# Linear attention and MoE on one core: w_in laid out by tiles, v loaded without its zero rows, and one folded step in another order of products

## The chip, the core and the metric

The kernel runs on one core of one Trainium2 chip. The metric is device time in microseconds: the median of 3 runs, 1050.9 us before the change (1047.07 to 1051.64).

## What is computed

```python
def phi(x):
    proj = np.einsum('bhsd,df->bhsf', x, w_phi)
    proj = proj - np.max(np.abs(proj), axis=-1, keepdims=True)
    return np.concatenate([np.exp(proj), np.exp(-proj)], axis=-1)
q_p, k_p = phi(q), phi(k)                       # q, k, v: 8 x 8 x 576 x 64
kv  = np.einsum('bhsf,bhsd->bhfd', k_p, v)
z   = np.sum(k_p, axis=2)
num = np.einsum('bhsf,bhfd->bhsd', q_p, kv)
den = np.einsum('bhsf,bhf->bhs', q_p, z)[..., None] + 1e-06
x   = (num / den).transpose(0, 2, 1, 3).reshape(4608, 512)
h   = x @ w_in                                  # 512 x 2048, float64
out = (h - np.tanh(h)) @ w_out                  # 2048 x 512, float64
```

## The kernel before

The program has two stages, both in an order written out by hand; the scheduler keeps it.

**Attention** (the first 290 us). Two heads of one batch form a unit, 32 units in all. `period(i)` works on unit i and finishes steps of units i-1 to i-4: projections of q and k (line 246), less their maximum (`t`, lines 257 and 260), exponentials, `kv` products (line 305), numerator and denominator (361, 376), transposes (270), and on the way the decoding of one weight tile from its 8-byte floats (`dec_0` to `dec_3`). SP issues nearly all loads and stores, in the order of the program: in a period the load of q and k (`qk`, line 229), in some periods the store of a split w_out tile (`wod`, 108) and of a decoded w_in tile (`wdi`, 520), then the reciprocal of the denominator (`rr`, 404), the load of v (233), a raw weight tile (`raw`, 175 or 180), the finished x (`xs`, 419) and the spread of the reciprocal over partitions (two `rb`, 411). One DMA of the period is issued by ACT: `den_recip_load`, `dn<-dd` (395), which stands behind the copy `kv` (342) and one exponential (283), and ahead of the next period's `t` (260).

Every DMA has one of eight completion counters, DMAHW0 to DMAHW7. They are taken in turn in the order of the program, by SP's and ACT's DMAs alike, and a DMA is issued only when the last one on its counter has landed (the wait is left out where an earlier wait of the same engine implies it). A period has eight DMAs, nine with a `wdi` store, ten with a `wod` store as well.

In the v load the array `v5` has 5 blocks of 128 rows; the first 64 rows of block 0 are zeros, and each load brings all 128 x 640 values into a buffer from a pool of two. A w_in load brings a tile of 512 x 128 values, in 512 pieces of 1,024 bytes; a w_out load brings 128 rows of 4,096 bytes.

**MoE** (from 290 us on). 9 groups of 512 tokens, 8 steps each, so steps 0 to 71. Steps 0 to 15 (`plain`) multiply directly. From step 16 on the step is folded: seven smaller products (`product`, line 791) into the PSUM banks W, V, Y and X are combined by additions on DVE. `q(old)` and `q(one)` are the output products (lines 713 and 719) of sets finished before: `high` uses `gh`, `low` uses `gl`, which POOL makes. The flag `joined` puts the products 3 and 2 (into Y) ahead of `q(old)` and product 4 (into X) behind `q(one)`; without it they stand between the two:

```python
joined = s > NP * FOLD and s != NS - 1
if joined:
    for n in (3, 2):
        product(r[n], g, j, n)
```

NP * FOLD is 16, so step 16 is not joined, and steps 17 to 70 are.

Of the kernel before, what the change touches and what calls it, by code (L numbers as in the profile page):

```python
# [8 lines left out]
F32 = mybir.dt.float32  # L9
# [10 lines left out]
P = 128  # L20
# [12 lines left out]
def tile_linear_attention_moe(  # L33
# [10 lines left out]
    nc = tc.nc  # L44
    B, H, S, D = dims
    F = w_phi.shape[1]
    DM, DFF = w_in.shape
    NHP = H // 2
    NJ = S // P
    SM = NJ * P  # L50
    SR = S - SM
# [3 lines left out]
    TPP = 2 * S // P  # L55
    PC = 2 * S
    NCT = DM // P
    NF = DFF // P
    CH = S // 2
    NP = NF // 2  # L60
    GT = 4
# [16 lines left out]
    xs = [dram.tile([NHP, P, S], F32, name=f"xs{b}") for b in range(B)]  # L78
    wod = [dram.tile([P, 2, DM], F32, name=f"wod{f}") for f in range(NF)]

# [5 lines left out]
    EARLY = [t for k in range(NO) for t in (("i", 2 * k), ("o", k), ("i", 2 * k + 1))]  # L86
    LATE = [("i", f) for f in range(NI, NF)] + [("o", f) for f in range(NO, NF)]
    NE = len(EARLY)
    SEQ = [t for e, l in zip(EARLY, LATE) for t in (e, l)] + LATE[NE:]
    wd = {f: dram.tile([P, DM], F32, name=f"wdi{f}") for f in range(NI)}  # L90
    HOME = {("i", f): f for f in range(NI, NF)} | {("o", f): f - NI for f in range(NI, NF)}

# [51 lines left out]
    with ExitStack() as c1:  # L144
        raw = c1.enter_context(tc.tile_pool(name="raw", bufs=2))
        p1 = c1.enter_context(tc.tile_pool(name="p1", bufs=1))
        p2 = c1.enter_context(tc.tile_pool(name="p2", bufs=2))
# [21 lines left out]
        def dec_load(n):  # L169
            u = Dec()  # L170
            u.side, u.f = SEQ[n]
            u.nm = f"{u.side}{u.f}"
            u.r = raw.tile([P, DM], U64, tag="raw", name=f"raw{u.nm}")
            if u.side == "i":
                nc.sync.dma_start(
                    u.r.rearrange("p (c f) -> p c f", f=P),
                    w_in[:, u.f * P : (u.f + 1) * P].rearrange("(c p) f -> p c f", p=P),
                )
            else:
                nc.sync.dma_start(u.r, w_out[u.f * P : (u.f + 1) * P, :])  # L180
            return u
# [39 lines left out]
        def load(u):  # L221
            u.qk = p2.tile([P, PC], F32, tag="qk", name=f"qk{u.i}")
            cuts = [(0, PC)]
            if u.i < 2:
                cuts = [(4 * P, PC), (0, 4 * P)]
            if u.i == 0:
                cuts = [(4 * P, 5 * P), (5 * P, PC), (0, 4 * P)]
            for o, w in cuts:
                nc.sync.dma_start(u.qk[:, o:w], qkT[u.i][:, o:w])

        def load_v(u):
            u.v = p2.tile([P, 5, 2, D], F32, tag="v", name=f"v{u.i}")
            nc.sync.dma_start(u.v.rearrange("p j e d -> p (j e d)"), v5[u.i])

        ROUNDS = ((4,), (5, 6, 7, 8), (0, 1, 2, 3))

# [185 lines left out]
        for i in range(B * NHP):  # L422
            u = Unit()
# [3 lines left out]
        NU = len(units)  # L427
        assert NU == 2 * NF
        load(units[0])
        wph = p1.tile([P, F], F32, name="wph")  # L430
        nc.scalar.dma_start(wph[0:D, :], w_phi)
        nc.scalar.dma_start(wph[D:P, :], w_phi)
        load(units[1])
        load_v(units[0])
        dec = [dec_load(0), dec_load(1)]
        def unit(i):
            return units[i] if 0 <= i < NU else None
# [169 lines left out]
    with ExitStack() as c2, tc.manual_schedule():  # L607
# [6 lines left out]

        for f in range(NF):
            if f not in hl:
# [10 lines left out]
        FOLD = 2  # L627
        steps = [(g, j) for g in range(NG) for j in range(NP)]
        NS = len(steps)
# [119 lines left out]
        def wo_fetch(g, j):  # L749
            for f in (2 * j, 2 * j + 1):  # L750
                wo[g, f] = wo_load(f)
# [31 lines left out]
        def product(o, g, j, n):  # L783
            h, l = weights(j, n)
            x = xc[g][n]
            i = 0
            for c in range(2):
                k = slice(c * P, (c + 1) * P)
                m = slice(c * HN, (c + 1) * HN)
                for w, a in ((h, 0), (h, 1), (l, 0)):  # L790
                    nc.tensor.matmul(o, w[:, k], x[:, a, m], start=(i == 0), stop=(i == 5))  # L791
                    i += 1
# [91 lines left out]
        def do(s, where):  # L884
            for fn, args in jobs.pop((s, where), ()):
                fn(*args)
# [3 lines left out]
        for k, ts in enumerate(LOWS):  # L890
            for t in ts.split():
                t = t[0], int(t[1:])
                job(k, "a1", split_hi, *t)
                job(k + 1, "v0", split_lo, *t)
        for j in range(NP):
            s = NP + j
# [45 lines left out]
        for s in range(NS + 3):  # L942
            one, two, old = sets.get((s - 1, 0)), sets.get((s - 1, 1)), sets.get((s - 2, 1))
            g, j = steps[s] if s < NS else (None, None)
            fold = g is not None and g >= FOLD
            if s >= NS:
                two = None
            begun = two is not None and steps[s - 1][0] < FOLD
            do(s, "d")
            if g is not None:  # L950
                Y, X = (ps_x.tile([P, GN], F32, tag=t, name=f"y{s}" if a == 0 else f"x{s}") for a, t in enumerate("yx" if fold or s % 2 else "wv"))
                if g:
                    wo_fetch(g, j)
                new, nxt = (Set(s, a, h, (2 * j, 2 * j + 1) if fold else (2 * j + a,), (2 * a, 2 * a + 1) if fold else (0, 1, 2, 3)) for a, h in enumerate((Y, X)))
                sets[s, 0], sets[s, 1] = new, nxt
            if fold:
                W, V = (ps_x.tile([P, GN], F32, tag=t, name=f"{t}{s}") for t in "wv")
                r = {1: W[:, lo_], 6: W[:, hi_], 2: Y[:, lo_], 3: Y[:, hi_], 4: X[:, lo_], 5: V[:, lo_], 7: V[:, hi_]}
                K = gp.tile([P, 3, HN], F32, tag="k", name=f"k{s}")
                u3 = K[:, 2, :]  # L960
                for n in (1, 6, 5, 7):
                    product(r[n], g, j, n)
                nc.scalar.copy(K[:, 0, :], r[1])
                joined = s > NP * FOLD and s != NS - 1
                if joined:
                    for n in (3, 2):
                        product(r[n], g, j, n)
            elif g is not None:
                plain(Y, g, 2 * j)
            if s != NS - 1:  # L970
                q(old)
            finish(2)
            do(s, "a")
            if not begun:
                run(two, "mk_")
            finish(4)
            run(two, "d3", "d4")
            if not fold:
                run(two, "d5")
            do(s, "v0")  # L980
            do(s, "d1")
            do(s, "p0")
            if fold:
                tt(u3, r[6], K[:, 0, :], ALU.add)
                tt(K[:, 1:3, :], V.rearrange("p (a n) -> p a n", a=2), u3.unsqueeze(1).broadcast_to([P, 2, HN]), ALU.add)
                if not joined:
                    for n in (3, 2):
                        product(r[n], g, j, n)
                    if s == NS - 1:
                        q(old, (0,))  # L990
                    product(r[4], g, j, 4)
                    if s == NS - 1:
                        q(old, (1,))
            elif g is not None:
                plain(X, g, 2 * j + 1)
            q(one)
            if fold:
                tt(Y, Y, K[:, 0:2, :].rearrange("p a n -> p (a n)"), ALU.add)  # L998
                tt(X[:, hi_], r[5], u3, ALU.add)
                if joined:  # L1000
                    product(r[4], g, j, 4)
                else:
                    tt(r[4], r[4], u3, ALU.add)
                run(two, "d5")
            if g is not None:
                run(new, "y_", "s1_", "s2_")
            run(two, "gh_", "gl_")
            if g is not None:
                run(new, "th_", "mk_", "d1", "d2")
                if fold and joined:  # L1010
                    tt(r[4], r[4], u3, ALU.add)
                if (s, "p1") in jobs:
                    nc.gpsimd.tensor_copy(mark, new.s1[:, 0:1])
                    do(s, "p1")
                run(new, "d3", "d4", "d5")
                do(s, "v1")
                if s == NS - 1:
                    nxt, end = (Set(s, f"1{k}", X[:, cols], (2 * j + k,), (2, 3), k == 1) for k, cols in enumerate((lo_, hi_)))
                    sets[s, 1], sets[s + 1, 1] = nxt, end
                run(nxt, "y_", "s1_", "s2_")  # L1020
                run(new, "gh_", "gl_")
                run(nxt, "th_", "d1", "d2")
                if not fold or s == NS - 1:
                    run(nxt, "mk_")
                if s == NS - 1:
                    run(nxt, "d3", "d4", "d5")
                    run(end, "y_", "s1_", "s2_")
                    run(nxt, "gh_", "gl_")
                    run(end, "th_", "mk_", "d1", "d2", "d3", "d4", "d5", "gh_", "gl_")
            do(s, "v")  # L1030
            do(s, "a1")
# [56 lines left out]
```

## Time and profile before

| | us |
|---|---|
| median of 3 runs | 1050.9 |
| the profiled execution | 1050.99 |
| its span, first to last instruction | 1049.2 |
| PE busy | 1030.6 (98%) |
| DVE, ACT, POOL busy | 935.3, 860.8, 486.7 |

The span is what the profile's rows divide; the execution's own time is 1.8 us longer. TensorE's granted clock is 0.999 of full speed over the span. Times in rows count from the span's start. PE is the matmul row of TensorE, PEld its weight loads; SPq and ACTq are the queues' own instructions, such as DMA issues.

### The profile page before, as it was taken

What the parts mean: (1) busy time and instruction counts of PE and PEld (TensorE: products, weight loads), DVE (VectorE), ACT (ScalarE), POOL (GpSimd) and SP (SyncE); (2) the same over time, 40 slices, a digit from 0 to 9 for tenths busy, and PEclk for the clock granted to TensorE, in tenths of its full rate; (3) what the DMA queues carried; (4) which work ended last, traced back from release to release, by engine and by line L of the source; (5) the groups of instructions that cost most, each with busy time, mean ns of one, the idle gap of its engine ahead of it and who ended that gap; (6) DMA issues with size and microseconds to landing.
All of it is one profiled execution on the core that took longest, in us unless ns stands there. A gap on an engine that the chain in (4) does not pass through costs nothing.

```text
span 1049.2 us, 24806 instructions
## 1 busy us (share of the span) xinstructions
PE 1030.6 (98%) x9476; PEld 855.8 (82%) x9476; DVE 935.3 (89%) x1457; ACT 860.8 (82%) x1580; POOL 486.7 (46%) x347
## 2 busy tenths in 40 slices
PE   8999999999999999999999999999999999999997
PEld 5666666666678888888989898999989898999986
DVE  7999999998989989998888888888888888888886
ACT  6999999998988877778878778777878777877766
POOL 4555555555324434434443553553463553553232
PEclk9999999999999999999999999999999999999999
DMA  6788888888633363343325325234325324332423
GB/s 206 205 269 245 259 248 266 248 258 249 190 117 124 116 222 125 101 138 105 119 97 185 109 93 201 82 121 162 120 93 188 109 94 154 129 121 81 161 89 112
DMA packets 76214, 165.55 MB, mean 158 GB/s; under 512 B 16704, under 2 KB 31296, under 8 KB 76096
## 3 DMA queue, kind: packets, MB, share of 16 engines
q1 hardware_dynamic: 71896, 163.63, 48.5%
q8 instruction: 75, 1.23, 0.5%
q10 hardware_dynamic: 4200, 0.34, 0.3%
q14 instruction: 43, 0.35, 0.1%
HBM read 134.28 MB, written 29.51 MB: 156 GB/s over the span
## 4 chain that ended last, share of the span: by engine, by line
PE 79%; DVE 9%; ACT 6%; DMA 4%; issue 1%; ACTq 0%; SPq 0%; DVEq 0%; POOL 0%; POOLq 0%
PE po L713 22%; PE po L719 11%; PE y L791 7%; PE w L791 7%; PE v L791 7%; PE pp L305 5%; PE po L361 4%; PE x L791 4%; PE y L800 3%; PE x L800 3%; PE pp L376 2%; ACT qe L283 1%; DMA rb<-rr 1%; DVE m L251 1%; ACT t L260 1%
## 5 line engine op out<-in xcount | busy, mean ns | idle before, releaser
L686 POOL TENSOR_TENSOR gl<-s,gh 128x512 fp32r<-128x512 f32 x144 | 223.6, 1553 | 417.7 <-ACT gh L682 297.5
L713 PE MATMUL po<-wo,gh 128*128 128x512 f32 x1152 | 302.5, 391 | 1.0 <-ACT gh L682 1.0
L713 PEld LDWEIGHTS po<-wo,gh 128*128 128x128 f32 x1152 | 211.8, 188 | 44.0 <-ACT gh L682 2.3
L719 PE MATMUL po<-wo,gl 128*128 128x512 f32 x576 | 169.9, 389 | 0.0
L647 ACT ACTIVATE y<-y 128x512 f32<-128x512 f32 x72 | 43.2, 600 | 114.5 <-DVE y L998 108.8
L315 POOL TENSOR_TENSOR ss<-kp 128x1024 f32<-128x1024 f32 (+1 forms) x32 | 73.6, 2299 | 118.3 <-DVE rb L416 89.9
L678 DVE COPY_PREDICATED s<-mk,th 128x512 f32<-128x512 uint32 x144 | 118.6, 823 | 9.5 <-ACT s L651 0.5
L719 PEld LDWEIGHTS po<-wo,gl 128*128 128x128 f32 x576 | 108.0, 188 | 22.6 <-DVE gl L686 0.2
L666 DVE SCALAR_TENSOR_TENSOR s<-s,y 128x512 f32<-128x512 f32 x144 | 99.5, 691 | 29.3 <-ACT s L651 29.2
L669 DVE SCALAR_TENSOR_TENSOR s<-s,s 128x512 f32<-128x512 f32 x144 | 104.1, 723 | 15.3 <-ACT gh L682 0.5
L651 ACT ACTIVATE s<-y,bias_t 128x512 f32<-128x512 f32 x144 | 104.2, 723 | 14.3 <-DVE s L672 9.3
L663 ACT ACTIVATE mk<-y,bias_t 128x512 f32<-128x512 f32 x144 | 103.7, 720 | 0.0
L655 ACT ACTIVATE s<-y,bias_t 128x512 f32<-128x512 f32 x144 | 101.9, 708 | 0.0
L251 DVE TENSOR_REDUCE m<-pp 128x8 f32<-128x1024 f32 (+1 forms) x96 | 90.8, 952 | 11.2 <-PE pp L246 9.9
L295 ACT ACTIVATE kp<-t 128x1024 f32<-128x1024 f32 (+1 forms) x128 | 87.6, 733 | 8.7 <-DVE t L257 7.9
L682 ACT CAST gh<-s 128x512 fp32r<-128x512 f32 (+1 forms) x145 | 88.4, 610 | 7.3 <-DVE s L678 4.6
L791 PE MATMUL y<-xc,hl 128*128 128x256 f32 x672 | 85.4, 275 | 1.1 <-DVE th L675 1.1
L791 PEld LDWEIGHTS y<-xc,hl 128*128 128x128 f32 x672 | 80.5, 188 | 1.3 <-issue 1.2
L305 PE MATMUL pp<-kp,v 128*32 128x256 f32 x1240 | 73.3, 381 | 7.7 <-ACT t L260 5.9
L257 DVE TENSOR_TENSOR t<-pp,m 128x1024 f32<-128x1024 f32 x64 | 78.4, 1225 | 2.3
L791 PE MATMUL w<-xc,hl 128*128 128x256 f32 x560 | 79.9, 277 | 0.0
L246 PE MATMUL pp<-wph,qk 64*128 64x128 f32 x1152 | 74.4, 277 | 1.6 <-issue 1.2
(142 smaller groups left out, 2187.5 us busy)
## 6 DMA issues: line engine op xcount, KB each, us to landing
wo<-wod SPq DMA_DIRECT2D x128, 512.0 KB
qk<-in_qkT SPq DMA_DIRECT2D x30, 576.0 KB
v<-in_v SPq DMA_DIRECT2D x32, 320.0 KB
rb<-rr SPq DMA_DIRECT2D x64, 144.0 KB
xs<-rb SPq DMA_DIRECT2D x32, 288.0 KB
out<-xco SPq DMA_DIRECT2D x35, 256.0 KB
rawi<-in_moe_w_in SPq DMA_DIRECT2D x16, 512.0 KB
rawo<-in_moe_w_out SPq DMA_DIRECT2D x16, 512.0 KB
```

The lines of the kernel that those rows point to most:

```text
L251: nc.vector.tensor_reduce(u.m, u.x, AX.X, ALU.max, apply_absolute_value=True, negate=True)
L305: nc.tensor.matmul(u.pc[o : o + HD, 0 : 2 * F], u.v[:, j, e, h * HD : (h + 1) * HD], u.kp[:, e, j, :, :], start=(a == 0), stop=(a == 4))
L651: nc.scalar.activation(self.s1, self.y, AF.Square, bias=bias_t[:, 0:1])
L655: nc.scalar.activation(self.gs, self.y, AF.Square, bias=bias_t[:, 1:2])
L663: nc.scalar.activation(self.mk, self.y, AF.Relu, bias=bias_t[:, 2:3])
L666: stt(self.s1, self.s1, PC1, self.y, ALU.add, ALU.mult)
L669: stt(self.s1, self.gs, PC2, self.s1, ALU.add, ALU.mult)
L678: nc.vector.copy_predicated(self.gs, self.mk.bitcast(U32), self.th)
L686: (nc.vector if self.spare else nc.gpsimd).tensor_tensor(self.gl, self.gs, f32(self.gh), ALU.subtract)
L713: nc.tensor.matmul(po[g, t], v.gh[:, cut], wo[g, f][:, k, :], start=not begun, stop=False)
L719: nc.tensor.matmul(po[g, t], v.gl[:, cut], wo[g, f][:, 0, :], start=False, stop=last and f == v.fs[-1])
L791: nc.tensor.matmul(o, w[:, k], x[:, a, m], start=(i == 0), stop=(i == 5))
```

## The change

w_in is laid out on the host as 16 tiles of 128 x 512 values, so that a tile is one block of 128 rows of 4,096 bytes, in the order that the load wanted in SBUF before. v is loaded in two DMAs that leave out the 64 zero rows of block 0: rows 64 to 127 whole (64 x 640 values), rows 0 to 63 without block 0 (64 x 512). The buffers are two fixed tiles whose zero part POOL writes once, at the start. Step 17 is no longer joined.

```diff
-    DM, DFF = w_in.shape
+    NF, DM = w_in.shape[0], w_out.shape[1]
...
-                nc.sync.dma_start(
-                    u.r.rearrange("p (c f) -> p c f", f=P),
-                    w_in[:, u.f * P : (u.f + 1) * P].rearrange("(c p) f -> p c f", p=P),
-                )
+                nc.sync.dma_start(u.r, w_in[u.f])
...
         def load_v(u):
-            u.v = p2.tile([P, 5, 2, D], F32, tag="v", name=f"v{u.i}")
-            nc.sync.dma_start(u.v.rearrange("p j e d -> p (j e d)"), v5[u.i])
+            u.v = vb[u.i % 2]
+            t = u.v.rearrange("p j e d -> p (j e d)")
+            nc.sync.dma_start(t[SR:P, :], v5[u.i, SR:P, :])
+            nc.sync.dma_start(t[0:SR, 2 * D :], v5[u.i, 0:SR, 2 * D :])
...
+        vb = [p1.tile([P, 5, 2, D], F32, name=f"v{b}") for b in range(2)]
+        for t in vb:
+            nc.gpsimd.memset(t[0:SR, 0], 0.0)
...
-                joined = s > NP * FOLD and s != NS - 1
+                joined = s > NP * FOLD + 1 and s != NS - 1
...
-        "moe_w_in": inputs["moe_w_in"],
+        "moe_w_in": _np.asarray(inputs["moe_w_in"]).reshape(H * D // W, W, -1, W).transpose(2, 1, 0, 3).reshape(-1, W, H * D),
```

SP's DMAs of period 13 and the head of period 14, before, with the counters that each waits for:

```order
L229 DMA qk15_2118<-in_qkT 128x1152 [waits DMAHW5_49,PE_49]
L108 DMA wod1_81<-wo1_1800 128x1024
L520 DMA wdi3_105<-dwi3_2037 128x512 [waits DMAHW7_49]
L404 DMA rr10_2190<-rn10_2191 128x9 [waits DMAHW0_49,DVE_49]
L233 DMA v14_2195<-in_v5 128x640 [waits DMAHW1_49,PE_49]
L175 DMA rawi14_2202<-in_moe_w_in 128x4x128 [waits DMAHW2_49,DVE_49,Activation_49]
L419 DMA xs2_74<-rb9_2078 128x576 [waits DMAHW4_49,DMAHW3_49,DVE_49]
L411 DMA rb10_2241<-rr10_2190 64x576 [waits DMAHW0_49]
```

The same place with the change:

```order
L225 DMA qk15_2122<-in_qkT 128x1152 [waits PE_49]
L107 DMA wod1_81<-wo1_1804 128x1024 [waits DMAHW4_49]
L521 DMA wdi3_105<-dwi3_2041 128x512 [waits DMAHW5_49]
L402 DMA rr10_2194<-rn10_2195 128x9 [waits DMAHW6_49,DVE_49]
L230 DMA v0_146<-in_v5 64x640 [waits DMAHW7_49,PE_49]
L231 DMA v0_146<-in_v5 64x512 [waits DMAHW0_49]
L174 DMA rawi14_2206<-in_moe_w_in 128x512 [waits DMAHW1_49,DVE_49,Activation_49]
L417 DMA xs2_74<-rb9_2082 128x576 [waits DMAHW2_49,DVE_49]
L409 DMA rb10_2245<-rr10_2194 64x576 [waits DMAHW6_49,DMAHW3_49]
```

The DMA of `qk15` was on counter 5 and is now on 3; `wod1` was on 6 and is now on 4, and one more DMA stands between it and `xs2`.

ACT at the end of the same period, before (`dn11` is the DMA that ACT issues, `t14` the next unit's first instruction):

```order
L287 ACTIVATE qe12_2207<-ptr12_2208 128x2x64
L342 COPY kv12_2206<-ptk12_2210 128x384 [waits PE_49]
L283 ACTIVATE qe12_2207<-ptt12_2209 128x2x512
L395 DMA dn11_2239<-dd11_2181 128x1x9 [waits DMAHW5_49,Activation_49]
L260 ACTIVATE t14_0_2249<-pp14_0_2244,m14_0_2247 128x128 [waits DVE_49]
L283 ACTIVATE qe12_2207<-ptt12_2209 128x2x512
```

With the change:

```order
L285 ACTIVATE qe12_2211<-ptr12_2212 128x2x64
L340 COPY kv12_2210<-ptk12_2214 128x384 [waits PE_49]
L281 ACTIVATE qe12_2211<-ptt12_2213 128x2x512
L393 DMA dn11_2243<-dd11_2185 128x1x9 [waits DMAHW4_49,Activation_49]
L258 ACTIVATE t14_0_2253<-pp14_0_2248,m14_0_2251 128x128 [waits DVE_49]
L281 ACTIVATE qe12_2211<-ptt12_2213 128x2x512
```

The order is the same; `dn11` waited for counter 5, on which `qk15` was the last, and now waits for counter 4, on which `wod1` is.

PE in step 17, from the last V product on, before (y, x: the banks Y and X; po: output products):

```order
L791 MATMUL v_7124<-xc_7_6815,tl_6384 128x256
L791 MATMUL y_7117<-xc_3_6706,hl_2122 128x256 x6
L791 MATMUL y_7117<-xc_2_6377,hl_1480 128x256 x6
L713 MATMUL po_0_6292<-wo_6895,gh_1_7088 128x512 x2
L719 MATMUL po_0_6292<-wo_6895,gl_1_7090 128x512
L713 MATMUL po_1_6296<-wo_6895,gh_1_7088 128x512 x2
L719 MATMUL po_1_6296<-wo_6895,gl_1_7090 128x512
L713 MATMUL po_2_6300<-wo_6895,gh_1_7088 128x512 x2
L719 MATMUL po_2_6300<-wo_6895,gl_1_7090 128x512
L713 MATMUL po_3_6304<-wo_6895,gh_1_7088 128x512 x2
L719 MATMUL po_3_6304<-wo_6895,gl_1_7090 128x512
L713 MATMUL po_0_7191<-wo_6993,gh_0_7107 128x512 x2
```

With the change:

```order
L792 MATMUL v_7128<-xc_7_6819,tl_6388 128x256
L714 MATMUL po_0_6296<-wo_6899,gh_1_7092 128x512 x2
L720 MATMUL po_0_6296<-wo_6899,gl_1_7094 128x512
L714 MATMUL po_1_6300<-wo_6899,gh_1_7092 128x512 x2
L720 MATMUL po_1_6300<-wo_6899,gl_1_7094 128x512
L714 MATMUL po_2_6304<-wo_6899,gh_1_7092 128x512 x2
L720 MATMUL po_2_6304<-wo_6899,gl_1_7094 128x512
L714 MATMUL po_3_6308<-wo_6899,gh_1_7092 128x512 x2
L720 MATMUL po_3_6308<-wo_6899,gl_1_7094 128x512
L792 MATMUL y_7121<-xc_3_6710,hl_2126 128x256 x6
L792 MATMUL y_7121<-xc_2_6381,hl_1484 128x256 x6
L792 MATMUL x_7122<-xc_4_6601,th_6113 128x256 x2
```

The 12 output products moved ahead of the 12 products into Y, and the 6 into X, which stood behind the next set's output products before, now follow Y at once.

## Rows read from the trace of the kernel before

**Rows 1.** The page's first part: engine, busy us, share of the span, instructions.

```profile
PE 1030.6 (98%) x9476; PEld 855.8 (82%) x9476; DVE 935.3 (89%) x1457; ACT 860.8 (82%) x1580; POOL 486.7 (46%) x347
```

**Rows 2.** Waits of PE, first 290 us (total, times, longest), and one such gap.

```profile
PE pp L305 <- ACT t L260: 5.9, 6, 1.5
...
142.62 0.64 PE L305 MATMUL pp<-kp,v 128*32 128x256 f32 x8 [0.78 <-ACT t L260]
```

**Rows 3.** Timeline of ACT, a period without late transfers (start, length, instruction).

```profile
95.59 0.48 ACT L342 COPY kv<-ptk 128x384 f32<-128x384 f32 x1 [0.23 <-PE ptk L270]
...
97.01 0.62 ACT L260 ACTIVATE t<-pp,m 128x128 f32<-128x128 f32 x2
```

**Rows 4.** The chain that ended last, 116 to 138 us (start, length, what).

```profile
116.32 7.01 DMA qk<-in_qkT
...
123.41 0.54 ACTq L395
...
123.99 0.63 ACT t L260 x2
...
124.67 2.37 PE pp L305 x40
...
131.22 6.91 DMA dn<-dd
```

**Rows 5.** Timeline of ACT: kv copy and issue of dn in four other periods.

```profile
69.76 0.48 ACT L342 COPY kv<-ptk 128x384 f32<-128x384 f32 x1 [0.22 <-PE ptk L270]
69.90 0.54 ACTq L395 DMA_DIRECT2D dn<-dd  x1
...
121.50 0.48 ACT L342 COPY kv<-ptk 128x384 f32<-128x384 f32 x1 [0.21 <-PE ptk L270]
...
175.30 0.48 ACT L342 COPY kv<-ptk 128x384 f32<-128x384 f32 x1 [0.21 <-PE ptk L270]
175.57 0.54 ACTq L395 DMA_DIRECT2D dn<-dd  x1
...
227.80 0.48 ACT L342 COPY kv<-ptk 128x384 f32<-128x384 f32 x1 [0.21 <-PE ptk L270]
...
229.34 0.54 ACTq L395 DMA_DIRECT2D dn<-dd  x1
```

**Rows 6.** The page's DMA issues (count, KB each).

```profile
qk<-in_qkT SPq DMA_DIRECT2D x30, 576.0 KB
v<-in_v SPq DMA_DIRECT2D x32, 320.0 KB
...
wod<-wo SPq DMA_DIRECT2D x16, 512.0 KB
wdi<-dwi SPq DMA_DIRECT2D x8, 256.0 KB
```

**Rows 7.** Busy time by stretch; the last two columns are DMA share and GB/s.

```profile
104.32:112.91 8.59, 8.51 (x161) 5.91 (x159) 8.28 (x13) 8.10 (x17) 4.93 (x3) 1.00 0.87 252
158.12:166.70 8.58, 8.50 (x161) 5.90 (x159) 8.27 (x13) 8.07 (x17) 4.94 (x3) 1.00 0.85 246
...
120.40:129.00 8.60, 7.45 (x140) 5.39 (x140) 7.75 (x11) 7.28 (x16) 4.94 (x3) 1.00 0.92 317
```

**Rows 8.** Timelines of PE, DVE and POOL in steps 16 and 17.

```profile
471.20 0.28 PE L791 MATMUL v<-xc,tl 128*128 128x256 f32 x1
472.53 1.65 PE L791 MATMUL y<-xc,hl 128*128 128x256 f32 x12 [1.05 <-DVE th L675]
474.02 0.62 PE L713 MATMUL po<-wo,gh 128*128 128x512 f32 x2
...
476.77 0.62 PE L713 MATMUL po<-wo,gh 128*128 128x512 f32 x2
...
475.36 0.68 DVE L675 TENSOR_TENSOR th<-x,th 128x512 f32<-128x512 f32 x1
...
470.64 1.42 POOL L686 TENSOR_TENSOR gl<-s,gh 128x512 fp32r<-128x512 f32 x1 [6.08 <-ACT gh L682]
```

More of the change, by code (lines that the diff above doesn't have):

```diff
@@ L57, in tile_linear_attention_moe @@
     NCT = DM // P
-    NF = DFF // P
     CH = S // 2
```

## The prediction

> **What bounds the kernel now.** I read the page's busy shares first [rows 1]: TensorE (PE) is busy 98% of the span, with DVE and ACT at 82 to 89%. So time can only be won or lost where PE stands still, or where work is added to or taken from PE; the change adds and takes no PE work. Then the view of waits, to see where PE stands still: in the attention stage (the first 290 us) it loses 5.9 us in 6 gaps, all in front of the kv products of line 305, all ended by ACT's `t` of line 260 [rows 2]. In the MoE stage there is one gap of 1.05 us that the change touches [rows 8]. These two places are what the change can touch.
>
> Why does ACT come late in the attention stage? ACT itself issues one DMA in each period, `dn<-dd` (line 395), and an engine that waits before an issue does nothing else meanwhile. In a normal period ACT starts the copy `kv` at 95.59 and `t` at 97.01 [rows 3], 1.42 us later, with the issue of `dn` between them. The chain of waits shows the bad case [rows 4]: a `qk` load takes 7.01 us to land, only then (123.41) does ACT issue `dn`, `t` begins at 123.99, 0.58 us after that issue, and the products start 0.68 us after `t`. Nothing in the data makes `dn` wait for `qk`. The waits of the built program do: DMAs of SP and ACT take eight completion counters in turn, and each waits for the last DMA on its own counter. From these rows comes a **rule for the slack**: `dn` may be issued up to 1.42 - 0.58 = 0.84 us after the start of the `kv` copy for nothing; every later microsecond holds up PE by one. By it the wait up to 123.41 cost 123.41 - 121.50 - 0.84 = 1.07 us [rows 4, 5] of the 5.9.
>
> **The change, part by part.**
>
> *One DMA more in each period (v in two pieces).* Eight counters against eight DMAs per period meant that `dn` waited for the previous period's `dn`, long landed. Against nine it waits for the DMA that stood behind the previous `dn`: in a plain period the second `rb` instead of `dn`; where a `wdi` store is in the period, `qk` instead of the second `rb`; where both a `wod` and a `wdi` store are, `wod` instead of `qk`. The order rows show the last case for `dn11`: its counter was qk15's and is now wod1's. A plain period has room, and the waits of `v`, `rr` and `rb` on SP hold up SP alone, which issues ahead of need. The four periods with a `wod` store of 512 KB behind `qk` [rows 6] have none. At 317 GB/s, what the DMA engines moved in the stretch with the longest backlog [rows 7], 512 KB take 1.65 us. So `dn` goes 1.65 us later than the row where it now waits for `qk`, less the slack [rows 5]:
> - at 69.90: 69.90 + 1.65 - 69.76 - 0.84 = 0.95 us of new gap
> - at 123.41: the slack is already used up, so all 1.65
> - at 175.57: 175.57 + 1.65 - 175.30 - 0.84 = 1.08
> - at 229.34: 1.54 after the copy, the slack is used up: 1.65
>
> Together 5.3 us. Bounds for the 1.65: 0, if the store lands along with `qk`, and 2.5, if the 256 KB of the `wdi` store that follows [rows 6] are served in between.
>
> Two more late periods exchange `rb` for `qk`. A `qk` is 576 KB [rows 6], 1.86 us at the same rate: where `dn` had its slack, 1.86 - 0.84 = 1.0 is the most, where it had none 1.86, and nothing if `qk` lands before `dn` is wanted. I take +0.4 for each of the two, nearer to 0 since most backlogs there are without a `wod` store; bounds 0 and 1.9.
>
> *What the DMA queue is spared.* v: 320 KB per load [rows 6] become 288 KB; 32 KB at 317 GB/s are 0.10 us per period. w_in: the same 512 KB in 128 rows of 4,096 bytes instead of 512 of 1,024. Nothing before shows w_in in the new form, but w_out is loaded in that form: the w_in period from 104.32 moves 252 GB/s at a DMA share of 0.87, the w_out period from 158.12 moves 246 at 0.85 [rows 7], that is 290 and 289 GB/s for a full share. By this the row form is worth nothing; bounds: 0.4 us per load gained, and, since longer pieces beside the tiny pieces of `dn` could hold those up (one `dn` took 6.91 us to land [rows 4]), 0.4 lost. I take a gain of 0.1, near the rows. So 0.2 us less backlog in front of each critical landing: six of them, -1.2.
>
> On w_in the Trainium skill ("DMA: Bandwidth & Descriptors", Specifications) speaks against a gain: it puts the least size for line rate at 512 bytes, which 1,024-byte rows already exceed. By that rule alone the 0.1 would be 0 and the sum below 0.6 us higher; the two rows agree with it.
>
> *What new gaps give back.* While PE waits, the DMA queue drains. The gap of 0.78 us at 142.62 [rows 2] follows the wait at 123.41 by two periods, in the same backlog (the `dn` between them, 131.22, took 6.91 us to land [rows 4]); 1.65 us more of waiting before it should clear it: -0.8. The longest gap, 1.5 us [rows 2], follows the wait at 229.34 in the same way; I count half of it: -0.7.
>
> *Zero rows by memset.* Two small memsets on POOL at the start, one of them ahead of the identity matrix: POOL, busy 46% [rows 1], has the room; bounds 0 and 0.1 us. The first `v` in two DMAs: landing is wanted at the first kv products only, several microseconds later: 0.
>
> *The second folded step (step 17).* PE ends the V products at 471.20 + 0.28 = 471.48 and stands still for 1.05 us, until DVE has read the bank that the Y products overwrite [rows 8]. Now the 12 output products of the previous step come first. They took 476.77 - 474.02 = 2.75 us, the 12 Y products 474.02 - 472.53 = 1.49. The third output product needs `gl`, which POOL ends at 470.64 + 1.42 = 472.06; PE would come to it at 471.48 + 2.75/6 = 471.94: a new wait of some 0.15. Then 2.6 more and 1.49 of Y bring PE to about 475.9, where the product into X now stands ahead of the other output products; `th<-x` reads that bank until 475.36 + 0.68 = 476.04: another 0.25 with the signal's way. Gain 1.05 - 0.4, say 0.6 us (bounds 0 and 1.05). From step 18 on PE runs the same order as before, so the gain stays.
>
> **Sum**: 5.3 + 0.8 - 1.2 - 0.8 - 0.7 - 0.6 = +2.8. The profiled execution took 1050.99 us (its span 1049.2 and 1.8 around it), next to a median of 1050.9, so **1053.8 us**, 0.3% slower. A measurement of this kernel tells about 0.5%, 5.3 us, from no change: this forecast lies inside that.
>
> **Rivals.**
> 1. *The queue's relief wins (faster).* If w_in's long rows shorten the landings by over 1.5 us in the crowded periods, no `dn` waits long and the old gaps close too. For: the whole attention stage suffers from landings of 7 us. Against: the w_out row above. At best 5.9 + 0.6 off: 1044.5; halfway 1047.7.
> 2. *No give-back (slower).* The new waits stand and the old gaps too, because each backlog forms anew within a period (the DMA share is 0.85 to 0.92 [rows 7]). Then 5.3 + 2 x 1.1 - 0.6 = +6.9, 1057.9. It decides from the point where `wod` lands 1.65 us or more behind `qk`.
> 3. *The counters do not bite*, for instance since the DMA engines reach `wod` together with `qk`; what stays is step 17 and a little relief: 1050.4.
> 4. *The change does not do what it says* in step 17: waiting for `gl` and for X eats all of it. That is 0.6 us of the sum, 1054.4, and does not change the sign.
>
> **How the numbers follow.** Forecast with 4: 0.42; rival 1: 0.18; rival 2: 0.22; rival 3: 0.18. Below 1045.6 (faster by over 0.5%) lies only the best half of rival 1, 0.09; above 1056.2 lie most of rival 2 and the forecast's upper end, 0.26; between, 0.65. The range leaves out the best of rival 1 and the worst of rival 2: 1046.5 to 1059.
>
> **What would show it.** Right: PE's gaps before line 305's products number six to eight and sum to 8 to 10 us; ACT's issue of `dn` stands 2 to 3 us behind its `kv` copy in the four periods with a `wod` store; the chain of waits runs through `wod` there. Step 17: no gap before Y, two short ones before a `gl` product and before X. Wrong: `dn` goes right behind its copy everywhere (rival 1 or 3), or the DMA share of the attention stage falls by more than a few hundredths (rival 1).

## The result, and the profile after the change

The change makes the kernel slower: **1058.19 us** (median of 6 runs, 1055.66 to 1060.01) next to 1050.38 (1047.07 to 1051.64) of the kernel before, a ratio of 1.0081 with a 95% interval of 1.0061 to 1.0101. The forecast was 1053.8 in a range of 1046.5 to 1059, that is +2.8 us, and +7.8 was measured: the sign is right, the size is 5 us short. The profiled execution took 1059.41 us, its span is 1057.6, so 8.4 us longer than the one of before.

TensorE's share of busy time on the page is the same 98% as in [rows 1]. Only its busy time has grown, by 3.3 us for the same 9,476 products; the rows on the clock below say why:

```profile
PE 1033.9 (98%) x9476; PEld 857.3 (81%) x9476; DVE 936.7 (89%) x1457; ACT 860.9 (81%) x1580; POOL 486.6 (46%) x349
```

The view of waits of PE in the attention stage tells the two kernels apart (line, what ended the waits, total, times, longest; it answers to [rows 2], and line 303 is line 305 of before):

```profile
PE pp L303 <- ACT t L258: 11.7, 8, 2.5
```

5.8 us more than before, in front of the same products and ended by the same instruction. ACT's timeline shows why, here in the four periods with a `wod` store and in one of the two later ones (start, length, instruction, in brackets idle time and what is taken to have ended it):

```profile
69.42 0.48 ACT L340 COPY kv<-ptk 128x384 f32<-128x384 f32 x1 [0.22 <-PE ptk L268]
72.63 0.54 ACTq L393 DMA_DIRECT2D dn<-dd  x1
73.21 0.63 ACT L258 ACTIVATE t<-pp,m 128x128 f32<-128x128 f32 x2 [2.39 <-DVE t L255]
...
123.57 0.48 ACT L340 COPY kv<-ptk 128x384 f32<-128x384 f32 x1 [0.22 <-PE ptk L268]
126.39 0.54 ACTq L393 DMA_DIRECT2D dn<-dd  x1
126.97 0.63 ACT L258 ACTIVATE t<-pp,m 128x128 f32<-128x128 f32 x2 [2.00 <-DMA wod<-wo]
...
179.02 0.48 ACT L340 COPY kv<-ptk 128x384 f32<-128x384 f32 x1 [0.22 <-PE ptk L268]
181.13 0.53 ACTq L393 DMA_DIRECT2D dn<-dd  x1
...
232.17 0.48 ACT L340 COPY kv<-ptk 128x384 f32<-128x384 f32 x1 [0.22 <-PE ptk L268]
235.26 0.54 ACTq L393 DMA_DIRECT2D dn<-dd  x1
...
273.56 0.55 ACTq L393 DMA_DIRECT2D dn<-dd  x1
274.16 0.63 ACT L258 ACTIVATE t<-pp,m 128x128 f32<-128x128 f32 x2 [0.89 <-DMA qk<-in_qkT]
```

`dn` is issued 3.21, 2.82, 2.11 and 3.09 us behind the `kv` copy, and where `t` is shown it starts 0.58 to 0.60 us behind that issue, as in [rows 4]. Where the view names a releaser that could hold ACT here, it is the `wod` store, and in the later period `qk`: the DMAs that the prediction names. (At 73.21 it names DVE's `t`, another tile that ACT's `t` does not read.) The issue at 126.39 is that of `dn11`, which the order rows ahead of the prediction show waiting for `wod1`'s counter.

PE's timeline at the same places has something more. These are the products behind the waits, and one set without a wait (x40 stands for the 40 kv products of one period):

```profile
73.89 2.37 PE L303 MATMUL pp<-kp,v 128*32 128x256 f32 x40 [2.46 <-ACT t L258]
...
127.65 4.05 PE L303 MATMUL pp<-kp,v 128*32 128x256 f32 x40 [2.06 <-ACT t L258]
...
182.40 2.37 PE L303 MATMUL pp<-kp,v 128*32 128x256 f32 x40 [1.36 <-ACT t L258]
...
236.53 4.05 PE L303 MATMUL pp<-kp,v 128*32 128x256 f32 x40 [2.34 <-ACT t L258]
246.80 2.37 PE L303 MATMUL pp<-kp,v 128*32 128x256 f32 x40
...
265.38 2.37 PE L303 MATMUL pp<-kp,v 128*32 128x256 f32 x40 [1.48 <-ACT t L258]
274.84 2.37 PE L303 MATMUL pp<-kp,v 128*32 128x256 f32 x40 [0.96 <-ACT t L258]
```

The waits follow the issue of `dn` one to one: where it stands 3.21, 2.82, 2.11 and 3.09 us behind the copy, PE waits 2.46, 2.06, 1.36 and 2.34 us, 0.75 to 0.76 less each time. But twice the 40 products also take 4.05 us instead of 2.37. The busy times by stretch of those products say what happened (the third number from the end is the granted clock of TensorE):

```profile
127.65:131.70 4.05, 4.05 (x44) 2.15 (x48) 3.75 (x7) 3.32 (x4) 1.74 (x2) 0.58 0.88 276
236.53:240.60 4.07, 4.07 (x44) 2.12 (x48) 3.28 (x7) 3.33 (x4) 1.49 (x2) 0.58 0.88 268
73.89:77.90 4.01, 4.01 (x72) 2.37 (x76) 2.98 (x7) 3.98 (x7) 1.38 (x2) 1.00 0.88 258
```

After PE had stood still for 2.06 and 2.34 us its clock was 0.58 of full, mostly the lower of its two levels (1.2 instead of 2.4 GHz), and each time that cost 4.05 - 2.37 = 1.68 us more. No wait is written for it: PE counts as busy.

Step 17 is the second place that the change touches. PE's timeline after it:

```profile
480.09 0.28 PE L792 MATMUL v<-xc,tl 128*128 128x256 f32 x1
480.20 0.63 PE L714 MATMUL po<-wo,gh 128*128 128x512 f32 x2
481.31 0.50 PE L720 MATMUL po<-wo,gl 128*128 128x512 f32 x1 [0.48 <-POOL gl L687]
...
485.11 0.50 PE L792 MATMUL x<-xc,th 128*128 128x256 f32 x2
```

The gap of 1.05 us before Y [rows 8] is gone, a gap of 0.48 before the first product with `gl` has come, and before X, where the prediction had a second one, there is none.

### The profile page after: what moved, and what is told of

The parts are those of the page before. It is cut to its first block, busy times and chain, and to the rows that moved or that the text cites. A ratio compares the mean times of both kernels' runs of the same rounds, so it can differ in the third digit from the quotient of the medians.

```text
span 1057.6 us, 24840 instructions
## 1 busy us (share of the span) xinstructions
PE 1033.9 (98%) x9476; PEld 857.3 (81%) x9476; DVE 936.7 (89%) x1457; ACT 860.9 (81%) x1580; POOL 486.6 (46%) x349
## 4 chain that ended last, share of the span: by engine, by line
PE 47%; ACT 4%; DVE 2%; issue 1%; DVEq 0%; ACTq 0%
PE po L714 17%; PE po L720 8%; PE y L792 6%; PE w L792 6%; PE v L792 6%; PE x L792 3%; ACT gh L683 1%; ACT y L648 1%; ACT s L652 1%; ACT s L656 1%; ACT th L660 1%; DVE s L673 1%; DVE th L676 0%; DVE y L999 0%; DVE k L986 0%
## 5 line engine op out<-in xcount | busy, mean ns | idle before, releaser
L667 DVE SCALAR_TENSOR_TENSOR s<-s,y 128x512 f32<-128x512 f32 x144 | 101.7, 707 | 28.0 <-ACT s L652 28.0
L303 PE MATMUL pp<-kp,v 128*32 128x256 f32 x1240 | 76.7, 395 | 13.4 <-ACT t L258 11.7
```

The source lines that it names most:

```text
L667: stt(self.s1, self.s1, PC1, self.y, ALU.add, ALU.mult)
```

## The experiments

In all of them the theory is: ACT's issue of `dn` waits for whatever last took its completion counter, and one more DMA per period makes that a `wod` store or a `qk`. Ratios are to runs of the kernel before on the same chip, with their 95% intervals.

**Which part of the change it is.** v's split alone, on the kernel before:

```diff
...
+            u.v = vb[u.i % 2]
+            t = u.v.rearrange("p j e d -> p (j e d)")
+            nc.sync.dma_start(t[SR:P, :], v5[u.i, SR:P, :])
+            nc.sync.dma_start(t[0:SR, 2 * D :], v5[u.i, 0:SR, 2 * D :])
...
```

> Kernel before with v's split alone (two DMAs of v into fixed buffers, zero rows by memset); w_in's layout and step 17 as before. Theory (one DMA more per period turns the eight completion counters, so that ACT's dn waits for wod or qk, and two of the longer waits halve TensorE's clock for the next 40 products): all of the change's loss is here, 1057 to 1060 us, PE gaps before the kv products of 11 to 12 us in sum, dn issued 2 to 3 us behind the kv copy in the periods with a wod store. Rival (w_in's rows of 4,096 bytes or step 17 cause the loss): 1050 to 1051 us, gaps about 6 us.

1060.68 us, ratio 1.0115 (1.0099 to 1.0131). The split alone costs all that the change costs, if not more (the two intervals just overlap). And the changed kernel with the split undone:

```diff
-            nc.sync.dma_start(t[SR:P, :], v5[u.i, SR:P, :])
-            nc.sync.dma_start(t[0:SR, 2 * D :], v5[u.i, 0:SR, 2 * D :])
+            nc.sync.dma_start(t, v5[u.i])
...
```

> Changed kernel, but v comes in one DMA of all 128 rows again (fixed buffers kept, no memset); w_in's rows and step 17 as changed. Theory (counters): dn never waits for a wod store, 1049 to 1051 us, PE gaps before the kv products of 4 to 6 us. Rival (w_in's rows or step 17 cause the loss): 1057 to 1059 us.

1049.53 us, 1.0000 (0.9986 to 1.0015). w_in's long rows, the fixed buffers and step 17 together change nothing that can be measured. PE's waits in the attention stage of these two, first the split alone:

```profile
PE pp L307 <- ACT t L262: 11.5, 6, 3.2
```

then the change with one v:

```profile
PE pp L302 <- ACT t L257: 4.6, 8, 0.9
```

**Whether it is the counter or the transfer.** One small DMA more on the kernel before, with v in one piece:

```diff
             nc.sync.dma_start(u.v.rearrange("p j e d -> p (j e d)"), v5[u.i])
+            nc.sync.dma_start(spare[u.i % 2], v5[u.i, 0:2, 0:D])
...
```

> Kernel before plus one DMA of 512 bytes (2 rows of 256) behind each v, read by nobody; v in one piece with its zero rows, w_in and step 17 as before. Theory (counters): the number of DMAs is all that matters, so the loss of the change comes with it, 1057 to 1060 us, the same periods late. Rival (v's split costs by its pieces, by the memset or by arriving late): within 1 us of before, 1050 to 1051.5 us.

1059.63 us, 1.0101 (1.0078 to 1.0123). 512 bytes that nobody reads cost as much as the whole change. ACT's timeline of this kernel names `wod` too:

```profile
128.90 0.62 ACT L261 ACTIVATE t<-pp,m 128x128 f32<-128x128 f32 x2 [1.94 <-DMA wod<-wo]
...
183.40 0.62 ACT L261 ACTIVATE t<-pp,m 128x128 f32<-128x128 f32 x2 [2.15 <-DMA wod<-wo]
```

Now the reverse, the changed kernel with the same pieces, of which the second is issued by POOL. In the built program POOL's DMAs do not take the counters of SP and ACT ("every DMA" in the part ahead of the prediction is too wide), so there are eight per period again:

```diff
-            nc.sync.dma_start(t[0:SR, 2 * D :], v5[u.i, 0:SR, 2 * D :])
+            nc.gpsimd.dma_start(t[0:SR, 2 * D :], v5[u.i, 0:SR, 2 * D :])
```

> Changed kernel, but the second piece of v is issued by POOL, whose DMAs do not take SP's and ACT's eight counters; the pieces, their bytes, w_in's rows and step 17 stay as changed. Theory (counters): the rotation is that of before, dn never waits for a wod store, 1049 to 1051.5 us (POOL's issuing work may cost up to 1 of it). Rival (the DMA traffic itself, the smaller pieces of v or w_in's rows hold dn up): 1057 to 1059 us.

1049.85 us, 1.0013 (1.0002 to 1.0023), and in its profiled execution PE waits less than in the kernel before (which the median over ten runs does not turn into time):

```profile
PE pp L303 <- ACT t L258: 2.9, 5, 0.9
```

These four tie the loss to one DMA more on the eight counters: it comes with that DMA and goes with it, whatever it carries. In the built programs with nine DMAs, `dn5`, `dn11`, `dn17` and `dn23` wait for `wod`; in the two with eight they wait for `qk`, as before the change. One rival is left by the times alone: each DMA more also takes SP's own time to issue. The timelines answer it. In the changed kernel, with v's split alone and with the small DMA, all 18 waits of PE before the kv products (behind the first set, at 20 us) equal the time from the `kv` copy to the issue of `dn`, less 0.73 to 0.76 us. So PE lost what ACT was late with `dn`, and wherever the view of these three names a DMA ahead of `t`, it is the one that the built program has `dn` wait for.

**Whether a wait that holds no computing engine is harmless.** `dn` issued by SP:

```diff
-                    den_recip_load(p, nc.scalar)
+                    den_recip_load(p)
```

> Changed kernel, but SP issues dn, so that a wait for its counter (or for dd) holds SP's queue and not ACT. Theory: ACT's t is never held up, 1043 to 1050 us, PE gaps below 5 us. Rival (dn late on SP, and behind it rb, qk and v late): 1053 us or more, PE waits for rb's or qk's consumers.

1049.96 us, 1.0001 (0.9971 to 1.0031): the whole loss is gone with nine DMAs per period, all of them issued by SP, so that SP's issuing time is not what costs. But two things have changed at once. In the built program `dn` now stands ahead of both `rb`, one place earlier in the turn, so that in the four crowded periods it waits for `qk`, as in the kernel before, and it is the first `rb` that waits for `wod` (SP's waits name it once, 0.9 us). What a `dn` that waits for `wod` would cost on SP, this run does not show. And nothing beyond the loss is gained. In DVE's waits there is now:

```profile
DVE rn L401 <- DMA dn<-dd: 5.8, 9, 1.3
```

ACT is not held, but `dn` comes late all the same, and DVE, which takes its reciprocal ahead of the maxima that `t` needs, waits for it. The other way to take ACT's `t` out from behind the wait, issuing `dn` after `t`:

```diff
-                    den_recip_load(p, nc.scalar)
                     later.append(lambda: q_exp(c, 1, q))
+                    later.append(lambda: den_recip_load(p, nc.scalar))
...
```

> Changed kernel, but ACT issues dn behind the t and q exponentials of the next period's start instead of before them; dn still waits for qk or a wdi store by the counters (worse than in the changed kernel). Theory (a waiting dn costs only because t stands behind it on ACT): t is never late, PE gaps before the kv products fall from 11.7 us below 5, no halved clock, 1043 to 1050 us. Rival (what counts is that dn itself comes late, through rr and rb): as slow as the changed kernel or slower, 1057 us or more, with the gaps at other products.

1058.76 us, 1.0093 (1.0059 to 1.0127). Here the time is the rival's, but PE's gaps, 9.1 us, still stand before the kv products, and after one of them, of 2.79 us, the 40 products took 4.01 us. By its new place `dn` waits for `qk` or `wdi` in every period from `dn1` to `dn23`, so more than the place of `t` has changed, and what that alone is worth the run does not show. DVE's waits for `dn` have grown to more than twice those above:

```profile
DVE rn L401 <- DMA dn<-dd: 13.9, 15, 3.1
```

**Which DMA the counter belongs to.** `qk` and the stores moved behind `rr` on SP, so that `dn` waits for a second `rb`, an `xs` store or the `dn` before:

```diff
-            if i + 2 < NU:
-                load(units[i + 2])
-            while stores:
-                stores.pop(0)()
...
             if r:
                 den_recip(r)
+            if i + 2 < NU:
+                load(units[i + 2])
+            while stores:
+                stores.pop(0)()
```

with v in two DMAs and in one:

> Changed kernel with all its nine DMAs per period, but SP's qk load and the wod and wdi stores are issued behind rr, so that dn's counter was last taken by a second rb, an xs store or the dn before, never by qk or a store of weights. Theory (which DMA stands eight places ahead of dn decides): PE gaps before the kv products below 4 us, 1044 to 1050 us. Rival (nine DMAs per period are too many, whatever their order): 1056 us or more.

> As the kernel above with qk and the stores behind rr, and v in one DMA again, eight per period: dn's counter was last taken by the dn before or by an xs store. Theory: the six late periods of the kernel before go too, since qk was what they waited for: attention ends 4 to 6 us earlier, 1044 to 1047 us. Rival (qk, issued some 5 us later, now comes late itself): PE waits at the projections, 1050 us or more.

1069.27 us (1.0190, 1.0154 to 1.0226) and 1069.13 (1.0181, 1.0145 to 1.0218): the theory misses. The times are those of the rivals, but not for their reasons: with nine and with eight DMAs the loss is the same, so it is not their number here, and PE does not wait at the projections but still before the kv products (25.3 and 20.5 us). What waits ahead of `t` is DVE, here in the first of the two:

```profile
DVE rb L414 <- DMA rb<-rr: 14.6, 10, 4.5
...
DVE rn L401 <- DMA dn<-dd: 9.2, 9, 2.2
```

The big transfers now stand just ahead of `dn` and `rb`, which I take to be why those land late; no run moved them without the counters. A chain `dn`, reciprocal, `rr`, `rb`, product runs through every period, and DVE and SP serve it in order; it is late either by a counter or by a backlog.

The next run was to set the counter right without moving anything, by four more small DMAs behind v, which makes `rr` the holder of `dn`'s counter in every period:

```diff
+            for n in range(4):
+                nc.sync.dma_start(spare[u.i % 2][:, n], v5[u.i, 0:2, 0:16])
...
```

> Changed kernel plus four more DMAs of 128 bytes per period behind v (read by nobody): 13 DMAs in a plain period, 15 with wod and wdi. By the rotation dn's counter was then last taken by rr in every period, a transfer of a few KB, and never by qk, wod or wdi. Theory (which DMA stands eight places ahead of dn decides, not how many there are): though it does more, it is faster than the changed kernel, 1047 to 1053 us, no gap over 1.5 us before the kv products, no halved clock. Rival (each DMA more makes it slower): 1065 us or more, since one small DMA more cost 10 us.

1074.82 us, 1.0241 (1.0219 to 1.0263): the time that the rival gave. Of the 24 us some 7.6 are the clock: five sets of the 40 products took 3.55 to 4.04 us instead of 2.37. ACT's timeline shows the counter at work, though (`rr` is what ended the wait), and SP's beside it, in the second fence, why I was wrong to call `rr` harmless:

```profile
186.95 0.48 ACT L342 COPY kv<-ptk 128x384 f32<-128x384 f32 x1 [0.21 <-PE ptk L270]
190.01 0.53 ACTq L395 DMA_DIRECT2D dn<-dd  x1
190.59 0.62 ACT L260 ACTIVATE t<-pp,m 128x128 f32<-128x128 f32 x2 [2.23 <-DMA rr<-rn]
```

```profile
181.39 0.54 SPq L225 DMA_DIRECT2D qk<-in_qkT  x1
181.99 0.42 SPq L107 DMA_DIRECT2D wod<-wo  x1
182.46 0.42 SPq L524 DMA_DIRECT2D wdi<-dwi  x1
183.60 0.57 SPq L404 DMA_DIRECT2D rr<-rn  x1
...
186.31 3.20 SPq L233 DMA_DIRECT2D spare<-in_v  x4
```

`rr` moves 4.5 KB, but it was issued at 183.60 behind 1.3 MB of `qk`, `wod` and `wdi`, and `dn`, which waited for it, went at 190.01, 6.4 us later. The four small DMAs also take SP itself 3.20 us here; SP's waits name `wod` for their line in four places:

```profile
SPq L233 <- DMA wod<-wo: 5.4, 4, 1.7
```

By these rows the rule is about time, not kind: with more DMAs per period, the one eight places ahead was issued more recently, and is less likely to have landed.

**Attempts at a faster kernel.** `dn` on SP and DVE's reciprocal later, behind the decoding, so that a late `dn` holds up nothing (the load of v, which follows `rr` on SP, moves with it):

```diff
-            if r:
-                den_recip(r)
...
-            if i + 1 < NU:
-                load_v(units[i + 1])
...
                 gate[i] = decode(w)
...
+            if r:
+                den_recip(r)
+            if i + 1 < NU:
+                load_v(units[i + 1])
...
```

with one v and with two:

> Changed kernel with v in one DMA, dn issued by SP (where its wait holds no engine that computes), and DVE's reciprocal of dn placed behind the decoding of the period's weights, so that dn has some 2 us more to land. Theory (with dn off ACT, the gaps left are DVE waiting for dn ahead of the maxima that t needs): DVE's waits for dn and PE's gaps before the kv products go below 2 us, 1044 to 1048 us. Rival (the later reciprocal makes rr, rb and then the product with rb late): 1050 us or more, with DVE waiting for rb.

> The same with v in two DMAs as in the changed kernel. Theory: where the wait for a counter holds SP alone, one DMA more per period costs nothing: within 1.5 us of the kernel with one v, 1044 to 1048 us. Rival (the second DMA of v costs by itself): 3 us or more behind it.

1062.69 us (1.0113, 1.0098 to 1.0128) and 1070.52 (1.0181, 1.0156 to 1.0206). DVE's waits for `dn` are down to 1.5 us, and the next step of the chain is late instead (with one v):

```profile
DVE rb L413 <- DMA rb<-rr: 15.7, 12, 2.6
...
DVE rn L400 <- DMA dn<-dd: 1.5, 1, 1.5
```

The rival holds in both; and the second DMA of v costs 7.8 us here, between the two medians, though its wait holds SP alone. SP is in the chain as well: it issues `rr` and `rb`.

Last, one v and the weight stores issued by POOL, after which `dn`'s counter is the last `dn`'s in all but the first and the last few periods:

```diff
-                    stores.append(lambda w=w: nc.sync.dma_start(wd[w.f], w.w))
+                    stores.append(lambda w=w: nc.gpsimd.dma_start(wd[w.f], w.w))
```

(`wod` likewise.)

> Changed kernel with v in one DMA, and the wod and wdi stores of the attention stage issued by POOL, outside the eight counters: SP and ACT issue eight DMAs in every period, so that dn's counter was last taken by the dn before in each of them; never by qk, as it still was in the periods with both stores. Theory: no wait on ACT ahead of dn's issue; what is left is DVE waiting for a late dn or rb, 2 to 4 us in sum: 1045 to 1049 us, at most 0.4% faster than before. Rival (the gaps left come from late landings, not from the counters; or POOL, held by the stores, is late with its sums): 1050 us or more.

1056.85 us, 1.0075 (1.0057 to 1.0092); the profiled execution, 1051.94, was the fastest of its six, so its rows are not those of a typical one. From 60 us on `dn` is issued within 0.14 us of its `kv` copy, but for one at 248.26 (`dn25`, 1.38 us behind; before the change it stands 1.62 behind), and still, on ACT, POOL and DVE (three fences, in this order):

```profile
61.67 0.53 ACTq L392 DMA_DIRECT2D dn<-dd  x1
```

```profile
59.79 0.61 POOL L107 DMA_DIRECT2D wod<-wo  x1 [0.80 <-DVE wo L210]
62.04 0.55 POOL L518 DMA_DIRECT2D wdi<-dwi  x1 [1.64 <-PE pp L243]
```

```profile
69.47 0.22 DVE L400 RECIPROCAL rn<-dn 128x9 f32<-128x9 f32 x1 [1.80 <-DMA dn<-dd]
```

`dn` was issued right behind its `kv` copy, and the reciprocal that waits for it starts 7.8 us later. The view of DMAs from 58 to 72 us has the landings (the last number, us from issue):

```profile
wod<-wo POOLq DMA_DIRECT2D x1, 512.0 KB, 5.0
...
rb<-rr SPq DMA_DIRECT2D x2, 144.0 KB, 7.6
wdi<-dwi POOLq DMA_DIRECT2D x1, 256.0 KB, 5.7
```

So the stores had landed at about 64.8 and 67.7, before the reciprocal could start, and `dn` landed in a backlog of which SP's `v`, raw tile, `xs`, `rb` and `qk` (issued from 59.66 to 64.00) are as much a part; which of them held it up is not shown. The Trainium skill ("DMA: Bandwidth & Descriptors", "Issuing engines are not separate DMA queues") says that DMAs of all engines run on the same 16 DMA engines, so that another issuing engine saves issue time alone. The trace agrees as far as it goes: with the stores issued by another engine `dn` is late all the same. The other five executions were 3.5 to 7.2 us slower than the profiled one. Their granted clock is 0.996 to 0.998 instead of 0.999; by an estimate from that difference and the span, 1 to 3 us of it are the clock, and the rest stays open. No kernel tried was faster than the one before.

## Why the prediction was right in sign and short in size

*The mechanism* was right at its place: eight counters, the DMA behind the previous `dn`, `t` 0.58 us behind the issue, PE one to one. The four experiments on v show it, with the waits, not only the order rows. The slack is 0.75 us instead of 0.84. PE's gaps number eight, as the prediction's signs had it, but sum to 11.7 us instead of 8 to 10.

*Four `wod` periods, +5.3.* PE's waits there are 2.46, 2.06, 1.36 and 2.34 us, 8.2 in sum. At the same places the kernel before had 1.15 and 0.78 and twice nothing, 1.9. So +6.3: near in sum, with each wait up to 1.5 us off its own term. At the first of them `dn` goes 3.07 us later behind its copy than before (3.21 instead of 0.14), past the bound of 2.5.

*Two `rb` to `qk` periods, +0.8.* They are the waits at 265.38 and 274.84, 1.48 and 0.96 us, 2.4 in sum. The forecast took a value near 0; the bound of 1.9 each holds.

*Queue relief, -1.2.* No run shows it. The kernel with v in one DMA and w_in's long rows is at 1.0000 of before, an interval that could by itself hide 1.2 us; with the second piece of v by POOL, which has the whole relief, it is 1.0013. In the four crowded periods together `dn` is issued 3.9 us behind its copies before the change, 4.8 in the first of these kernels and 2.4 in the second, in one execution each: that moves either way, and not by a steady 0.2 per landing. The term credited a shorter transfer as if nothing else decided when `qk` and `wod` land.

*Give-back, -1.5.* It came, and larger: the old gaps at 142.62, 195.41 and 249.16 (0.78, 0.85 and 1.46 us) are gone but for one of 0.16, so -2.9. Rival 2, which kept them, has the right total (1057.9) by the wrong route.

*The clock: not in the sum at all.* Two waits of over 2 us were followed by 1.68 us each of products at the lower clock, +3.4. This term, put at nothing, is the largest single error. The rows of before could not price it: no gap there was longer than 1.46 us, and behind none was the clock lower; I should have said that longer gaps than the trace holds were being forecast, and bounded their after-effect.

*Step 17, -0.6.* From the first products of each step in PE's timeline, PE takes 11.24 us for step 17 and 10.55 for step 18, 21.79 in sum, before 11.63 and 10.27, 21.90: -0.1. With the new order it is 21.75 with one v and 21.72 with POOL's piece, with the old order 22.06 with v's split alone and 22.02 with the small DMA, so the new order gains some 0.25. The wait for `gl` was 0.48 instead of 0.15, and step 18 takes 0.28 longer, for which I had counted nothing.

The waits and the clock make 6.3 + 2.4 - 2.9 + 3.4 = 9.2; the first kv product starts 0.36 us earlier than before (19.72 instead of 20.08), and with step 17 that is 8.7, next to a span that is 8.4 longer; the other 0.3 I did not trace. That the time still lies in the range is in part luck: the larger give-back took back 1.4 us of what the other terms fell short by. Rival 1 (relief) fell with the 1.0000 above, and rival 3 (counters do not bite) with the small DMA.

## What to carry to other kernels

Where DMAs share a few completion counters in turn, adding one, or moving one to another engine and so to another place, changes what the later ones wait for: list, for each DMA on a computing engine, which transfer holds its counter and how long ago that was issued. Before splitting a load, count the DMAs of a period; 512 bytes in a DMA of their own cost 10 us here, and the split, which saves 32 KB per load, cost no less. And a small transfer that a later instruction needs is as late as the backlog it is issued into: taking its wait away from one engine (ACT) only showed the next one (DVE, then SP).

## What was not expected of the hardware

A wait of TensorE can cost more than its length. In the changed kernel and in the one with v's split alone there are six waits of over 2 us before the kv products (2.06 to 3.24 us); after four of them the next 40 products took 3.96 to 4.05 us instead of 2.37, after two they did not, and after none of the shorter waits. The later kernels show that the length of the wait alone does not decide. In the one with `qk` behind `rr` and one v, and in the one with v's split and the late reciprocal, there are:

```profile
103.51 2.37 PE L302 MATMUL pp<-kp,v 128*32 128x256 f32 x40 [3.16 <-ACT t L257]
```

```profile
141.19 4.05 PE L303 MATMUL pp<-kp,v 128*32 128x256 f32 x40 [1.92 <-ACT t L258]
```

The Trainium skill ("TensorE: Matmul & The Clock Gate", Part 1) has the clock fall to 1.2 GHz after PE was idle; that agrees with the granted 0.58. What decided between 3.16 us without and 1.92 us with a fall these runs do not tell, and no run kept PE busy in a gap to try it.
